# Moving the value products of the segment's tokens behind its Wo pass, with new PSUM banks for K and for the extra transposes

## Chip, cores, metric

One core of one Trainium2 chip. The metric is device time in microseconds (us), median of the runs. All runs quoted here, apart from the single look at a synthetic kernel, were in the fast state: a granted TensorE clock of 0.99 to 1.00, and times of one kernel on one chip that agree within 0.8%. The profiler's trace of one execution of each run is what the views below show.

## The reference, cut to what matters

A pre-LN block: an attention part A with a recurrent memory, then a gated feed-forward part B. Part A goes through 64 segments of 32 tokens in order. Each segment is put behind 8 memory rows; the attention's first 8 output rows are the memory of the next segment. That is the recurrence which the kernel cannot break.

```python
for s in range(n_seg):                       # 64 segments, 32 heads of 128, model width 640
    h = concatenate([mem, x[:, 32*s:32*s+32]])        # 8 + 32 rows
    q, k, v = h @ Wq, h @ Wk, h @ Wv                  # per head
    p = softmax(where(mask, q @ k.T * scale, -1e9))
    o = (p @ v) @ Wo                                  # summed over heads
    mem = o[:, :8]                                    # into the next segment
    outs.append(o[:, 8:])
h  = x + concat(outs)                        # A works on layernorm(x)
h2 = h + reglu_ffn(layernorm(h))             # part B
```

## The kernel before, the parts that matter

Every operation is recorded in one list with the tiles and PSUM banks that it reads and writes; a solver sets the semaphores. Each engine executes its operations in the order of the list, so the order of the text is the order of the engine. Key `B(n)` is a PSUM bank; two users of one bank are always ordered, readers among themselves too.

```python
BQ = (0, 1); T0, T1 = 2, 3; P0, P1, P2, P3 = 4, 5, 6, 7          # names of the 8 banks

def project(act, akeys, j, halves, banks, chunks=range(5)):      # j: 0 Q, 1 K, 2 V
    # 5 chunks x 4 column groups: a 128x32 stationary load, then a matmul of 512 columns
    # (one load serves two matmuls where both halves are asked for)

def to_act(s, wkey, src):        # memory rows of the next segment: Wo's result -> stationary operand
    add("dve", transpose(TBf, src)); add("dve", tensor_copy(act_r[..., 0:M], TBf))

def pv_x(s, b0):                 # "x values": 64 loads + 64 matmuls on 32x32 tiles
    for kh in range(2):
        for a in range(2):
            for c in range(4):
                for g in range(4):
                    pe.matmul(bank(b0 + g)[32*c:32*c+32, 129*kh:129*kh+129], Px[...], t[...])
def norm_x(b0):                  # VectorE: reciprocal (rx), two multiplies (ox), reads banks b0..b0+3

def extra_units(s):              # 3 of 4 segments also project 32 extra tokens, in pieces ("filler")
    ...
    def fin():                   # for K or Q: transposes of the result, in the next segment
        trans8(tok[2], ("tok", 2), tok[3], ("tok", 3), P0)
        (evac_k if j == 1 else evac_q)(P0, t0, 32, 0, "act")

for s in range(64):
    ...
    if s > 0:
        project(a, ks, 1, (0,), (P2,)); to_tok(P2, 0, "act")     # K, needs the memory rows
        project(a, ks, 1, (1,), (P3,)); to_tok(P3, 1, "dve")
        if fin: fin()
        pv_x(s - 1, BQ[0]); norm_x(BQ[0])                        # x values of the segment before
        ... row_scale ...
        project(a, ks, 0, (0, 1), (P0, P1)); ...                 # Q
        project(a, ks, 2, (0,), BQ[:1]); ...                     # V, first half
        trans8(... P2); trans8(... P3)                           # K and Q transposed
        project(a, ks, 2, (1,), (T0,)); ...                      # V, second half
    scores(s); exp_mem(); exp_x()                                # 64 loads + 64 matmuls, then ScalarE
    filler(0); pv_mem(s); filler(1); trans_om(s); trans_ox(s - 1, T0)
    wo_pass(oT[par], ..., T1)                                    # 128 loads + 128 matmuls, 160 columns
    to_act(s + 1, B(T1), bank(T1)[:, 0:160])
    ...
    filler(2)                                                    # extra projection or Wo of memory rows
    if evac: evac()
    ... row_stats ...
```

The softmax here doesn't subtract the row's maximum and nothing guards it: scores larger than these inputs give would overflow.

## Time and profile before

| | before |
|---|---|
| time, median of 3 | 1268.34 us (1266.53 to 1270.35) |
| span, profiled run | 1262.6 us |
| TensorE busy | 1176.5 us, 93% |
| TensorE idle for the memory copy (act_r), segments only | 12.6 us in 47 waits |
| TensorE idle for the evacuation of the extra transposes | 13.8 us in 30 waits |

The head of the page of the kernel before, and its queue of instruction transfers:

```profile
span 1262.6 us, 64636 instructions
## 1 busy us (share of the span) xinstructions
PE 1176.5 (93%) x31431; PEld 661.4 (52%) x29111; DVE 611.0 (48%) x1497; ACT 408.4 (32%) x775; POOL 26.6 (2%) x94
...
q8 instruction: 237, 3.88, 1.3%
```

PE is TensorE's matmuls, PEld its weight loads, which overlap (1176.5 and 661.4 us busy in a span of 1262.6).

The waits of TensorE in the segments, 60 to 1046 us (columns: total, times, longest):

```profile
PE ps L345 <- DVE act_r L467: 12.6, 47, 0.7
PE ps L345 <- ACT Qr L378: 7.1, 15, 0.6
PE ps L345 <- ACT Kr L378: 6.7, 15, 0.5
...
PE ps L546 <- issue: 1.7, 4, 0.6
```

L345 is the projections. The first line is K waiting for the memory rows, the next two are Q waiting for bank 4 while ScalarE reads the extra transposes from it. TensorE's timeline shows both in one segment (columns: start, duration, instruction, in brackets the idle time before it and what ended it):

```profile
301.69 0.73 PE L546 MATMUL ps<-Wo,oT 128*32 128x160 bf16 x32
302.24 0.39 PE L345 MATMUL ps<-W,act_e 128*32 128x512 bf16 x4
302.46 0.39 PE L331 MATMUL ps<-W,act_e 128*32 128x512 bf16 x4
303.09 2.34 PE L345 MATMUL ps<-W,act_r 128*32 128x512 bf16 x40 [0.24 <-DVE act_r L467]
305.36 0.62 PE L364 MATMUL ps<-ident,tok 128*128 128x128 bf16 x8
305.91 0.28 PE L583 MATMUL ps<-Vr,Px 32*32 32x129 bf16 x16
...
307.10 0.40 PE L345 MATMUL ps<-W,act_r 128*32 128x512 bf16 x4 [0.45 <-ACT Qr L378]
```

Order: end of the Wo pass (L546), filler (act_e), wait, K, extra transposes (L364), x values (L583), wait, Q.

### The profile page before, as it was taken

What the parts mean: (1) busy time and instruction counts of PE and PEld (TensorE: products, weight loads), DVE (VectorE), ACT (ScalarE), POOL (GpSimd) and SP (SyncE); (2) the same over time, 40 slices, a digit from 0 to 9 for tenths busy, and PEclk for the clock granted to TensorE, in tenths of its full rate; (3) what the DMA queues carried; (4) which work ended last, traced back from release to release, by engine and by line L of the source; (5) the groups of instructions that cost most, each with busy time, mean ns of one, the idle gap of its engine ahead of it and who ended that gap; (6) DMA issues with size and microseconds to landing.
All of it is one profiled execution on the core that took longest, in us unless ns stands there. A gap on an engine that the chain in (4) does not pass through costs nothing.

```text
span 1262.6 us, 64636 instructions
## 1 busy us (share of the span) xinstructions
PE 1176.5 (93%) x31431; PEld 661.4 (52%) x29111; DVE 611.0 (48%) x1497; ACT 408.4 (32%) x775; POOL 26.6 (2%) x94
## 2 busy tenths in 40 slices
PE   0889999999999999999999999999999997999998
PEld 0255555555556555555555555555555554455454
DVE  2244545454545454555555555454545442543522
ACT  0323333333333333333333333333333321321311
POOL 1000000000000000000000000000000000000000
PEclk9999999999999999999999999999999998999999
DMA  9801000010110101010111010100000025110100
GB/s 364 310 21 24 21 23 21 23 23 22 23 24 21 25 19 25 21 44 19 43 22 44 21 44 20 24 20 23 20 21 20 19 99 183 37 63 22 43 21 21
DMA packets 47819, 60.03 MB, mean 48 GB/s; under 512 B 20224, under 2 KB 36288, under 8 KB 47552
## 3 DMA queue, kind: packets, MB, share of 16 engines
q1 hardware_dynamic: 43520, 45.41, 12.6%
q10 hardware_dynamic: 4032, 10.49, 2.2%
q8 instruction: 237, 3.88, 1.3%
q14 instruction: 30, 0.25, 0.1%
HBM read 36.79 MB, written 6.55 MB: 34 GB/s over the span
## 4 chain that ended last, share of the span: by engine, by line
PE 86%; DMA 4%; DVE 4%; ACT 3%; issue 1%; SPq 1%; POOL 0%; DVEq 0%; ACTq 0%; POOLq 0%
PE ps L345 32%; PE ps L546 12%; PE ps L331 9%; PE ps L884 9%; PE ps L364 6%; PE ps L912 5%; PE ps L488 3%; PE ps L372 2%; PE ps L558 2%; PE ps L521 2%; DVE TBf L466 2%; DMA W<-in_A_Wk_dram 2%; PE ps L583 2%; ACT Kr L378 1%; ACT Qr L378 1%
## 5 line engine op out<-in xcount | busy, mean ns | idle before, releaser
L345 PE MATMUL ps<-W,act_r 128*32 128x512 bf16 x6460 | 447.2, 381 | 39.0 <-DVE act_r L467 12.6
L345 PEld LDWEIGHTS ps<-W,act_r 128*32 128x32 bf16 x6460 | 162.9, 96 | 286.0 <-issue 84.4
L380 DVE CAST tok<-ps 128x512 bf16<-128x512 f32 x161 | 110.9, 689 | 154.8 <-PE ps L345 78.3
L378 ACT ACTIVATE tok<-ps 128x512 bf16<-128x512 f32 x161 | 95.9, 596 | 229.7 <-PE ps L331 187.8
L546 PE MATMUL ps<-Wo,oT 128*32 128x160 bf16 x8448 | 163.8, 236 | 3.1 <-issue 2.6
L546 PEld LDWEIGHTS ps<-Wo,oT 128*32 128x32 bf16 x8448 | 148.6, 98 | 12.7 <-issue 4.5
L331 PE MATMUL ps<-W,act_r 128*32 128x512 bf16 x1420 | 138.8, 381 | 0.0
L364 PEld LDWEIGHTS ps<-ident,tok 128*128 128x128 bf16 x1288 | 72.2, 98 | 48.5 <-issue 24.2
L364 PE MATMUL ps<-ident,tok 128*128 128x128 bf16 x1288 | 89.1, 220 | 4.7 <-DVE tok L380 4.7
L604 ACT ACTIVATE oT<-ps 128x768 bf16<-128x768 bf16 x64 | 51.9, 811 | 124.4 <-PE ps L372 124.4
L345 PE MATMUL ps<-W,act_e 128*32 128x512 bf16 x900 | 89.6, 381 | 0.1
L331 PE MATMUL ps<-W,act_e 128*32 128x512 bf16 x900 | 89.2, 379 | 0.0
L378 ACT ACTIVATE Qr<-ps 128x512 bf16<-128x512 bf16 (+3 forms) x110 | 69.1, 658 | 57.4 <-DVE Qr L380 45.4
L596 DVE TENSOR_TENSOR ox<-ps,rx 128x512 bf16<-128x512 f32 x128 | 82.4, 685 | 2.2
L899 DVE TENSOR_TENSOR hT<-g,ps 128x512 bf16<-128x512 bf16 (+1 forms) x56 | 37.8, 686 | 74.7 <-PE ps L884 53.1
L466 DVE STREAM_TRANSPOSE TBf<-ps 128x160 f32<-128x160 f32 x64 | 22.4, 350 | 100.7 <-PE ps L546 100.6
L884 PE MATMUL ps<-xn2T,Wu 128*128 128x512 bf16 x260 | 66.7, 388 | 4.2 <-DMA Wu<-in_B_W_up_dram 4.2
L884 PE MATMUL ps<-xn2T,Wg 128*128 128x512 bf16 x260 | 66.6, 388 | 3.1 <-ACT g L897 3.1
L912 PE MATMUL ps<-Wd,hT 128*128 128x320 bf16 x448 | 68.1, 300 | 0.0
L378 ACT ACTIVATE wtok<-ps 128x160 bf16<-128x160 f32 x64 | 19.5, 304 | 138.7 <-DVE TBf L466 122.4
L897 ACT ACTIVATE g<-ps 128x512 bf16<-128x512 f32 (+1 forms) x56 | 32.3, 594 | 97.1 <-PE ps L884 97.1
L380 DVE CAST Vp<-ps 128x512 bf16<-128x512 f32 x64 | 44.3, 692 | 27.8 <-PE ps L345 26.4
(88 smaller groups left out, 1169.5 us busy)
## 6 DMA issues: line engine op xcount, KB each, us to landing
Vr<-Vp SPq DMA_DIRECT2D x124, 48.8 KB
xt<-in_A_x_dram SPq DMA_DIRECT2D x30, 160.0 KB
Vr<-Vp SPq DMA_DIRECT2D x128, 32.5 KB
attn_d<-wtok SPq DMA_DIRECT2D x256, 7.5 KB
W<-in_A_Wk_dram ACTq DMA_DIRECT2D x1, 2560.0 KB
W<-in_A_Wq_dram ACTq DMA_DIRECT2D x1, 2560.0 KB
W<-in_A_Wv_dram ACTq DMA_DIRECT2D x1, 2560.0 KB
Wo<-in_A_Wo_dram ACTq DMA_DIRECT2D x1, 2560.0 KB
```

Source lines behind the costliest of these rows:

```text
L331: return pe.add_instruction(mybir.InstMatmult(name=nc.get_next_instruction_name(), engine=mybir.EngineType.PE, ins=[pe.lower_ap(rhs), pe.l ...
L345: ins = pe.matmul(*a, start=(c == 0), stop=(c == DC - 1), skip_group_check=True)
L364: ins = pe.matmul(bank_bf(b)[:, k * 128:(k + 1) * 128], t[:, (k % 4) * 128:(k % 4 + 1) * 128], ident[:, :], is_transpose=True)
L378: add("act", lambda a: a.activation(dst, src, ACTF.Copy), r=r, w=w)
L380: add("dve", lambda v: v.tensor_copy(dst, src), r=r, w=w)
L466: add("dve", lambda v: v.transpose(TBf[:].rearrange("p c t -> p (c t)"), src), r=[wkey], w=[("TBf",)])
L488: i = pe.matmul(o, lh, Qr[:, h, q, :], start=True, stop=True, skip_group_check=True)
L546: i = pe.matmul(bank(bk)[32 * gg:32 * gg + 32, 0:160], src[:, hb, :], w[:, gg], start=(hb == 0), stop=(hb == 31), skip_group_check=True)
L596: add("dve", lambda v, kh=kh: v.tensor_tensor(ox[:, :, kh, :], src[:, :, kh, 0:128], ap(rx, kh, [[2, 4], [0, 128]]), ALU.mult), r=[B(b0 + ...
L604: add("act", lambda a: a.activation(oT[par][:, :, M:32].rearrange("p (k g) q -> p g k q", g=4), src[:, :, :, 0:RID], ACTF.Copy), r=[B(bk)] ...
L884: ins = pe.matmul(bank(bk), w[:, c, lo:lo + 128], xn2T[par][:, c, :], start=(c == 0), stop=(c == DC - 1))
L912: i = pe.matmul(bank(bk)[:, 0:320], hT[par][p0:128, j, u * 128:(u + 1) * 128], Wd[p0:128, j, hf * 320:(hf + 1) * 320], start=(j == 0), sto ...
```

## The change

Intent: fill the wait for the memory rows with the x values, which need nothing from them, and take the extra transposes off a bank that Q needs. Everything else follows from freeing banks. The whole diff:

```diff
--- before.py
+++ after.py
@@ -742,8 +742,8 @@
                     to_tok(BQ[i], 2 + i, e)
 
         def fin():
-            trans8(tok[2], ("tok", 2), tok[3], ("tok", 3), P0)
-            (evac_k if j == 1 else evac_q)(P0, t0, 32, 0, "act")
+            trans8(tok[2], ("tok", 2), tok[3], ("tok", 3), BQ[1])
+            (evac_k if j == 1 else evac_q)(BQ[1], t0, 32, 0, "act")
         return part, evac, (fin if j < 2 else None)
 
     EARLY = (31, 35, 39, 43)
@@ -780,22 +780,24 @@
         if s > 0:
             a, ks = pass_act(s)
             t0, nr = rider_tokens(s)
-            project(a, ks, 1, (0,), (P2,))
-            to_tok(P2, 0, "act")
-            project(a, ks, 1, (1,), (P3,))
-            to_tok(P3, 1, "dve")
+            project(a, ks, 1, (0,), (T0,))
+            to_tok(T0, 0, "act")
+            project(a, ks, 1, (1,), (T1,))
+            to_tok(T1, 1, "dve")
             if fin:
                 fin()
-            pv_x(s - 1, BQ[0])
-            norm_x(BQ[0])
+            if s % 4 == 2 and ln:
+                row_stats(xt, ("xt",), n_rows(nb))
+            if e2b is not None:
+                row_stats(xt, ("xt",), 128)
+            if not last:
+                project(a, ks, 0, (0, 1), (P0, P1))
+                to_tok(P0, 2, "act")
+                to_tok(P1, 3, "dve")
             if s % 4 == 2 and ln:
                 row_scale(xt, ("xt",), n_rows(nb), xt, ("xt",))
             if e2b is not None:
                 row_scale(xt, ("xt",), 128, at, ("at",))
-            if not last:
-                project(a, ks, 0, (0, 1), (P0, P1))
-                to_tok(P0, 2, "act")
-                to_tok(P1, 3, "dve")
             project(a, ks, 2, (0,), BQ[:1])
             to_v(BQ[0], Vp[par], 0, ("Vp", par), "act")
             trans8(tok[0], ("tok", 0), tok[1], ("tok", 1), P2)
@@ -854,17 +856,16 @@
         filler(2)
         if woe:
             copy_oTe(s - 1, T0)
+        pv_x(s, P0)
         if evac:
             evac()
+        norm_x(P0)
         if woe:
             woe_sum(BQ[0])
             woe_store(s // 4 - 1)
-        if s % 4 == 1 and ln:
-            row_stats(xt, ("xt",), n_rows(nb))
         if s % 4 == 3 and e2 is not None:
             add_attn(xt[:, :], xt, at, [("xt",), ("at",)], [("xt",)])
             dma(h_d[128 * e2:128 * e2 + 128, :], xt[:, :], r=[("xt",)], w=[("h_d", e2)])
-            row_stats(xt, ("xt",), 128)
 
 
     BG, BU, BD, BT = (0, 1), (2, 3), (4, 5), (6, 7)
```

## The prediction

> **What bounds the kernel.** TensorE: 1176.5 of 1262.6 us busy (first part of the page), 86% of the chain of waits. VectorE is 48% busy, ScalarE 32%. In the 64 recurrent segments (14.85 to 16.1 us, scores to scores in the timeline) TensorE idles at two places (its waits, 60 to 1046 us): key projection <- VectorE's memory transpose/copy (act_r), 12.6 us in 47 waits; query projection <- ScalarE's evacuation of the extra K/Q transposes, 7.1 + 6.7 us in 30; once <- VectorE's ox, 1.6 us.

> These understate the cost. [...] I measure from the last matmul start of one phase to the first start of the next: filler->K takes 0.62 us (0.43 after a Wo pass of the memory rows), x values->Q 0.67 where the extra transposes stand before it, against 0.15 where nothing is waited for. [...] here projection->x values costs 0.31, against 0.22 between four-matmul groups.

> **What the change does.** No arithmetic is added or removed. The 64 x-value matmuls (0.51 us, first to last start) move from behind K to in front of it, into the wait for act_r. The extra transposes go to bank 1, so Q on banks 4, 5 no longer waits for their 1.02 us evacuation. x values of 63 segments now use banks 4 to 7, so Q waits for the normalisation instead (0.21 + 1.29 us on VectorE), which has K's 2.2 us to hide in. K uses banks 2, 3. Layer-norm statistics (2 x 0.48 + 0.21 us) move behind it.

> **Cost by kind of segment** (filler to Q, excluding K itself and the extra transposes):
> - With extra transposes (30): before 0.62 + 0.15 + 0.51 + 0.67 = 1.95; after 0.31 + 0.51 + 0.155 + 0.15 = 1.125. Gain 0.82, 24.8 us in all.
> - After a segment with the Wo pass of memory rows (about 14): before 0.43 + 0.31 + 0.155, after 0.23 + 0.155 + 0.22. Gain 0.29, 4 us.
> - After a segment with extra V (15): nearly nothing. There VectorE's half of the V evacuation waits for ScalarE's (0.71 us idle before Vr in the timeline) and stands in front of the normalisation, which ends about 3.5 us after the filler's last start, where Q could start at 3.15. Q picks up a new wait of about 0.4 us, which eats the 0.40 gain.
> - First segments and the single long ox wait: about 3.5 us.

> Sum: 32 us, all on the critical path since TensorE sets the pace. 1268.3 - 32 = 1236 us. Range 1229 to 1246. Chances: faster by over 2% (under 1243) 0.84, within 2% 0.15, slower 0.01.

> **What would show it.** Waits of K on act_r and of Q on ScalarE's Kr/Qr evacuation both almost gone; a new wait of Q on ox, some 15 times, about 0.2 to 0.4 us; segments ending in s mod 4 = 3 and 0 falling from 16.05 and 15.92 to about 15.2 and 15.1, mod 2 from 15.1 to 14.8, mod 1 staying at 14.85. Feed-forward unchanged.

> **What would make it wrong.** VectorE running later than I lay out, so that Q waits for ox everywhere (30 more waits of 0.3 us cost 9 us); x values waiting at their new place; a lower granted clock (0.993 now); "issue" gaps turning up where waits were.

Two passages are cut from it, where the cuts are marked: the reason given for measuring from start to start, and a mechanism given for the step of 0.31 us. Neither was shown by a run of this case. The sum is 24.8 + 4 + 3.5 = 32.3, put down as 32, and the 0.31 and 0.22 us are measured in the trace before.

## The result and the profile after

The changed kernel took 1280.74 us (1277.19 to 1285.59, 4 runs) against 1267.65 us (4 runs): ratio 1.0101, 95% interval 1.0075 to 1.0128. It is slower by 1%, clear of the noise but inside the 2% either way that the prediction called "within 2%" and gave 0.15; 2.5% faster was forecast. A ratio here is that of the fast runs of the same rounds, as recorded, so it is not quite the ratio of the medians.

The head of the page after:

```profile
span 1279.7 us, 64704 instructions
## 1 busy us (share of the span) xinstructions
PE 1176.9 (92%) x31413; PEld 664.0 (52%) x29111; DVE 608.8 (48%) x1497; ACT 407.7 (32%) x775; POOL 26.6 (2%) x94
...
q8 instruction: 237, 3.88, 1.3%
```

Busy time is the same; the 17 us are idle time. TensorE's waits after, same window:

```profile
PE ps L583 <- issue: 31.2, 31, 1.7
PE ps L345 <- issue: 5.3, 10, 1.6
PE ps L546 <- issue: 4.4, 10, 0.9
PE ps L558 <- issue: 2.2, 2, 1.3
```

Both waits that the change was made against are gone, as forecast: no act_r, no Kr, no Qr in this window. In their place TensorE idles in front of the x values (L583) and elsewhere for "issue", the profile's word for waiting on nothing that it shows. The timeline after, for a segment of the same kind, shows where:

```profile
286.01 2.40 PE L546 MATMUL ps<-Wo,oT 128*32 128x160 bf16 x128
288.24 0.39 PE L345 MATMUL ps<-W,act_e 128*32 128x512 bf16 x4
288.45 0.39 PE L331 MATMUL ps<-W,act_e 128*32 128x512 bf16 x4
288.77 0.28 PE L583 MATMUL ps<-Vr,Px 32*32 32x129 bf16 x16
288.84 0.26 PE L583 MATMUL ps<-Vp,Px 8*32 8x129 bf16 x14
290.25 0.23 PE L583 MATMUL ps<-Vp,Px 8*32 8x129 bf16 x2 [1.15 <-issue]
290.25 0.28 PE L583 MATMUL ps<-Vr,Px 32*32 32x129 bf16 x16
290.32 0.41 PE L583 MATMUL ps<-Vp,Px 8*32 8x129 bf16 x16
290.66 2.34 PE L345 MATMUL ps<-W,act_r 128*32 128x512 bf16 x40
292.93 0.62 PE L364 MATMUL ps<-ident,tok 128*128 128x128 bf16 x8
293.48 0.40 PE L345 MATMUL ps<-W,act_r 128*32 128x512 bf16 x4
```

The gap falls in the middle of one recorded operation, after 30 of its 64 matmuls, where the program has no semaphore at all. Counting TensorE's instructions (loads, matmuls and the semaphore instructions between them) from the start of the trace and looking at the transfers of the instruction queue gives, for four of the gaps after:

```
gap ends   instruction number   modulo 256   last 16 KB instruction packet began   256 instructions before
258.66     11969                193          2.68 us earlier, took 1.46            3.50 us earlier
290.25     13762                194          2.30 us earlier, took 0.96            3.66 us earlier
322.01     15553                193          2.42 us earlier, took 0.92            3.64 us earlier
354.28     17346                194          2.32 us earlier, took 0.99            3.15 us earlier
```

Of the 67 issue gaps over 0.1 us in the whole trace, 58 stand at 193 or 194 modulo 256; the other nine lie in the feed-forward, where some matmul records are missing, so that the count is no longer exact. (Why 193 and not 0 is not shown; the count begins with the first recorded instruction, and all 22 issue gaps of the synthetic kernel below stand at 193 too.) All 58 end 1.2 to 1.6 us after the last 16 KB packet of the queue has ended. The queue moves 16 KB packets, 237 for TensorE's 60,848 instructions, that is one packet for 257. By these counts TensorE stands at the end of a block of 256 instructions and waits for the next.

How can the demand exceed the supply? Over a whole segment before (880 to 956 instructions in 14.85 to 16.1 us in most) 256 instructions take 4.1 us or more. But the Wo pass is 256 instructions in 2.2 us and the x values are 128 in 0.5 us (2.17 and 0.51 us from first to last matmul start, medians before). The change put them next to each other, with 32 or fewer instructions of filler between.

To weigh it, I took for every block end between 60 and 1046 us the step from one matmul start to the next, less the median of the same kind of step elsewhere, where it was larger than normal steps are. This sum is called the block-end loss below. It is 7.9 us before and 62.0 us after. The span grew by 17.1 us, so everything else became 62.0 - 7.9 - 17.1 = 37 us shorter; 32 us were forecast. This is a balance of one trace of each, and the fixed window leaves out the last segment of the slower kernel. Taken from the first scores to the last, the 63 steps grew by 15.0 us (984.7 to 999.7) and the loss from 8.1 to 64.1, which leaves 41 us. So 37 to 41 us is what the two counts give.

### The profile page after: what moved, and what is told of

It is laid out like the page before. It is cut to its first block, busy times and chain, and to the rows that moved or that the text cites. A ratio compares the mean times of both kernels' runs of the same rounds, so it can differ in the third digit from the quotient of the medians.

```text
span 1279.7 us, 64704 instructions
## 1 busy us (share of the span) xinstructions
PE 1176.9 (92%) x31413; PEld 664.0 (52%) x29111; DVE 608.8 (48%) x1497; ACT 407.7 (32%) x775; POOL 26.6 (2%) x94
## 4 chain that ended last, share of the span: by engine, by line
PE 89%; DMA 4%; issue 4%; DVE 1%; SPq 1%; ACT 0%; POOL 0%; DVEq 0%; ACTq 0%; POOLq 0%
PE ps L345 32%; PE ps L546 12%; PE ps L331 10%; PE ps L885 8%; PE ps L364 6%; PE ps L913 5%; PE ps L583 3%; PE ps L558 3%; PE ps L488 2%; PE ps L372 2%; PE ps L521 2%; DMA W<-in_A_Wk_dram 2%; SPq L304 1%; PE ps L533 1%; DMA Wd<-in_B_W_down_dram 1%
## 5 line engine op out<-in xcount | busy, mean ns | idle before, releaser
L345 PE MATMUL ps<-W,act_r 128*32 128x512 bf16 x6460 | 450.7, 383 | 14.5 <-DMA W<-in_A_Wk_dram 8.5
L345 PEld LDWEIGHTS ps<-W,act_r 128*32 128x32 bf16 x6460 | 166.8, 97 | 246.7 <-issue 103.3
L378 ACT ACTIVATE tok<-ps 128x512 bf16<-128x512 f32 x161 | 95.7, 595 | 234.8 <-PE ps L345 127.6
L546 PEld LDWEIGHTS ps<-Wo,oT 128*32 128x32 bf16 x8448 | 147.4, 97 | 17.1 <-issue 8.9
L331 PE MATMUL ps<-W,act_r 128*32 128x512 bf16 x1420 | 142.9, 385 | 0.0
L378 ACT ACTIVATE Qr<-ps 128x512 bf16<-128x512 bf16 (+3 forms) x110 | 69.2, 658 | 62.7 <-DVE Qr L380 45.5
L885 PE MATMUL ps<-xn2T,Wg 128*128 128x512 bf16 x250 | 62.5, 379 | 3.9 <-ACT g L898 2.5
L378 ACT ACTIVATE wtok<-ps 128x160 bf16<-128x160 f32 x64 | 19.5, 304 | 142.2 <-DVE TBf L466 125.2
L583 PE MATMUL ps<-Vp,Px 8*32 8x129 bf16 x2048 | 42.7, 222 | 20.3 <-issue 20.3
```

The source lines that it names most:

```text
L331: return pe.add_instruction(mybir.InstMatmult(name=nc.get_next_instruction_name(), engine=mybir.EngineType.PE, ins=[pe.lower_ap(rhs), pe.l ...
L345: ins = pe.matmul(*a, start=(c == 0), stop=(c == DC - 1), skip_group_check=True)
L378: add("act", lambda a: a.activation(dst, src, ACTF.Copy), r=r, w=w)
L546: i = pe.matmul(bank(bk)[32 * gg:32 * gg + 32, 0:160], src[:, hb, :], w[:, gg], start=(hb == 0), stop=(hb == 31), skip_group_check=True)
L583: i = pe.matmul(bank(b0 + g)[32 * c:32 * c + 32, 129 * kh:129 * kh + 129], Px[32 * g:32 * g + n, 256 * a + 32 * k:256 * a + 32 * k + 32], ...
L885: ins = pe.matmul(bank(bk), w[:, c, lo:lo + 128], xn2T[par][:, c, :], start=(c == 0), stop=(c == DC - 1))
```

## Experiments

| run | what | time us | before, same chip | ratio | block-end loss us |
|---|---|---|---|---|---|
| e2_after_shift128 | after, stream shifted by half a block | 1270.31 | 1264.24 | 1.0047 | 53.7 |
| e3_before_shift128 | before, shifted likewise | 1268.04 | 1267.91 | 1.0009 | 11.1 |
| e4_after_half_loads | after, 64 loads fewer in each Wo pass | 1234.18 | 1264.24 | 0.9755 | 17.3 |
| e5_before_half_loads | before, likewise | 1255.73 | 1264.24 | 0.9928 | 0 |
| e6_move_only | after, extra transposes back on bank 4 | 1307.01 | 1267.91 | 1.0311 | 51.4 |
| e1_fin_bank6 | before, extra transposes on bank 6 | 1255.15 | 1264.24 | 0.9924 | 9.7 |
| e8_bank6_stats | e1 with the statistics moved | 1256.25 | 1265.62 | 0.9915 | 15.9 |
| e9_split_memory | e8 with the memory copy in two pieces | 1251.25 | 1265.62 | 0.9882 | 17.7 |
| e10_k_joint | after, 20 loads fewer in each K | 1274.99 | 1267.26 | 1.0052 | 54.6 |
| e11_after_again | after, unedited | 1282.32 | 1267.26 | 1.0112 | 62.9 |

### The supply by itself

A kernel in which TensorE runs alone on zeros (result wrong on purpose; one run of 285.0 us, its state unknown, mean granted clock 0.927): stretches of 1024 loads and 1024 matmuls of 160, 224, 288 and 352 columns between slow stretches, then a burst in the form of the x values, then 160 columns again beside small DMAs.

```diff
+for N in (160, 224, 288, 352):        # each after 192 slow matmuls of 512 columns
+    for r in range(256):
+        for g in range(4):
+            pe.matmul(bank(b)[32*g:32*g+32, 0:N], oT[0][:, r % 32, :], wsrc[:, 0:N], ...)
+for r in range(32): ...               # 512 matmuls on 32x32 tiles, 129 columns
```

> TensorE alone (output zeros on purpose): stretches of load + matmul pairs whose matmuls stream 160, 224, 288 and 352 columns in four column groups, which unhindered need 2.2, 3.0, 3.9 and 4.7 us per 256 instructions, between slow stretches of 512 columns; then a burst like the x values (1.0 us per 256), then 160 columns again while small DMAs run. Supply theory: the 160-column stretch runs at a block time of 3.0 to 3.6 us in place of 2.2, 224 at the same, 288 and 352 at their own pace without gaps, the burst at 3.0 to 3.6 us per 256 after a first part that runs free, and 160 with DMA traffic somewhat slower, 3.3 to 4.0. Rival (no such limit; the gaps of the changed kernel are its own): 2.2 us for 160 columns, 1.0 for the burst.

The unhindered times in it are estimates: the Wo pass before, 160 columns, took 2.17 us for 256 instructions, which scaled by columns gives 2.2, 3.0, 3.9 and 4.8; the 1.0 of the burst is twice the 0.51 us of the x values.

The stretches in the view by groups (L321: 160 columns, L335: 224, L349: 288, L363: 352, L378: burst, L397: 160 with DMA traffic; columns: busy, mean ns, idle before):

```profile
L363 PE MATMUL ps<-Wo,oT 128*32 128x352 bf16 x1024 | 38.4, 313 | 0.0
L349 PE MATMUL ps<-Wo,oT 128*32 128x288 bf16 x1024 | 31.6, 286 | 0.0
L335 PE MATMUL ps<-Wo,oT 128*32 128x224 bf16 x1024 | 25.9, 259 | 2.9 <-issue 2.9
L321 PE MATMUL ps<-Wo,oT 128*32 128x160 bf16 x1024 | 19.2, 233 | 7.7 <-issue 7.7
L397 PE MATMUL ps<-Wo,oT 128*32 128x160 bf16 x1024 | 19.2, 233 | 8.5 <-issue 8.5
...
L378 PE MATMUL ps<-Vp,Px 32*32 32x129 bf16 x512 | 5.4, 250 | 7.3 <-issue 7.3
```

And the burst in the timeline:

```profile
184.45 1.52 PE L378 MATMUL ps<-Vp,Px 32*32 32x129 bf16 x159
188.24 1.26 PE L378 MATMUL ps<-Vp,Px 32*32 32x129 bf16 x128 [2.27 <-issue]
192.25 1.46 PE L378 MATMUL ps<-Vp,Px 32*32 32x129 bf16 x128 [2.74 <-issue]
195.97 1.16 PE L378 MATMUL ps<-Vp,Px 32*32 32x129 bf16 x97 [2.27 <-issue]
```

The first 159 matmuls and their loads run free; then exactly 128 matmuls, 256 instructions, come every 3.7 to 4.0 us, though they are busy for 1.3 to 1.5. The free part is 319 instructions in the trace, the 63 left of the current block and one more block. Stretches whose own pace is slower than that (288 columns: 3.9 us per 256, 352: 4.8) have no gap; 224 columns (about 3.1 on its own, worked out from the two slower stretches) is held at 3.6 on average, 160 columns (about 2.2, as in the Wo pass before) at 3.4, free first part included. These averages agree with the expectation, but the blocks that follow the free part do not quite: by the gaps in the trace they came every 3.45 to 3.73 us at 160 columns and every 3.45 to 4.00 us at 224, and those of the burst every 3.7 to 4.0 us, where 3.0 to 3.6 had been expected. (The granted clock was 0.76 in the window of the burst and 1.00 in the 160-column stretch; whether that lengthened the block times of the burst was not shown.) DMA traffic added 0.1 us per block on average, so contention is not the cause: the gaps are there with no other DMA running (from 184 to 197.2 us, the burst, the DMA view shows 4 packets, all of the instruction queue).

### Alignment

The same padding in front of both kernels, in time when TensorE idles anyway:

```diff
+def pad(pe):
+    for _ in range(64):
+        i = pe.matmul(bank(P3)[:, 0:32], ident[:, :], ident[:, 0:32], start=True, stop=True, ...)
+    return i
+add("pe", pad, r=[("ident",)], w=[B(P3)])
```

> The changed kernel with 128 more TensorE instructions (64 small matmuls on an unused bank) in the idle time before the weights arrive, so that every later TensorE instruction stands half a block of 256 further on in the instruction stream. Theory (instruction supply: blocks of 256 TensorE instructions arrive no faster than about one in 3.3 us, and the stretch Wo pass + filler + x values asks for more): the total stays at 1281 us within 8 us, and the issue gaps move from instruction count 193 modulo 256 to about 65 modulo 256. Rival (unlucky alignment of the blocks with the segments, which both repeat every 3584 instructions): the time falls to 1235 to 1255 us. Rival (the gaps are hidden waits for a semaphore or a DMA at the new place of the x values): the gaps stay at the same instructions of the segment and the time stays.

> The kernel before with the same 128 instructions in front. Supply theory: 1268 us within 6 us, its few issue gaps at about 65 modulo 256. Rival (the kernel before is fast by a lucky alignment): 1280 us or more.

> The changed kernel, unedited, on the same chip as the run beside it: ratio to before 1.010 as first measured (1.007 to 1.013), some 50 to 60 us of stalls at block ends. If the ratio falls to 1.005 here, the 7 us that the shift by 128 instructions seemed to win were the chip's.

The gaps of the shifted kernel stand at other instructions of the segments and, counted with the padding, still at 193 and 194 modulo 256 (the expectation's 65 holds only without counting it). The changed kernel lost 62.9 us at block ends unshifted (e11) and 53.7 us shifted; ratios 1.0112 (1.0074 to 1.0150) and 1.0047 (1.0018 to 1.0076), on two chips. My bound of 8 us around 1281 was missed: the shift is worth some 7 to 9 us in the changed kernel, though the two intervals just touch, and why is open. Alignment is not the cause of the loss: the shift did not bring the 1235 to 1255 us of that rival, most of the loss stays, and the kernel before does not care (1.0009).

The trace after settles this rival without any run. In it four segments are 3634 instructions in most cases (3643 in others), and not the 3584 of the expectation, which would be exactly 14 blocks. So the block ends move on by about 50 instructions every four segments, and one run meets many alignments in turn: the gaps in the x values stand anywhere between the matmul numbered 1 and the one numbered 62, counted from 0 to 63. (That the gaps in the list above are 1791 to 1793 instructions apart says only that each stands at a block end.) This also speaks against a hidden wait at one instruction of the x values.

### Fewer instructions in the burst

Every second group of loads is left out of the Wo pass (the arithmetic is wrong). Same matmuls, 64 of 256 instructions fewer.

```diff
     for gg in range(4):
+        if hb % 2:
+            i = again(pe, bank(bk)[...], src[:, hb - 1, :], w[:, gg], False, hb == 31, gg)   # no load
+            continue
         i = pe.matmul(bank(bk)[32 * gg:32 * gg + 32, 0:160], src[:, hb, :], w[:, gg], ...)
```

> The changed kernel with every second group of weight loads left out of the Wo pass (64 of its 256 instructions; result wrong on purpose; matmuls and their sizes as before). Supply theory: replaying the trace with those instructions taken out and a block per 3.2 to 3.4 us leaves 18 to 27 us of stalls in place of 46 to 59, so about 1252 us (1243 to 1262). Rival (hidden wait at the x values, or slower x values on banks 4 to 7): the gaps stay, 1275 us or more.

> Control: the same loads left out of the kernel before (result wrong on purpose). Supply theory: only the few stalls that the kernel before has go, 5 to 10 us: 1258 to 1264 us. If the loads themselves cost TensorE time, it falls by as much as the changed kernel does, 28 us, to about 1240.

TensorE's waits of the changed kernel without those loads, in the segments (L587 is the x values there):

```profile
PE ps L587 <- issue: 6.7, 13, 0.9
...
PE ps L345 <- issue: 1.0, 3, 0.4
PE ps L550 <- issue: 0.5, 1, 0.5
```

The changed kernel fell from 1.0101 of before, as first measured, to 0.9755, 1234 us; its span is 45.4 us shorter and its block-end loss 44.7 us smaller. The control lost 8.5 us, about what its block ends had cost (7.9). So by these two numbers the loads themselves cost TensorE almost nothing here; what they cost is their place in the stream. The time fell below the expected 1243 to 1262 us, so the range was missed: 17.3 us of block-end loss were left, just under what my replay gave (18 to 27 us), but it had started the changed kernel at 46 to 59 us, too low. This is also the strongest check of the forecast: with the supply relieved, the change is worth 1255.73 - 1234.18 = 21.6 us over the kernel before with the same loads left out, with 17.3 us still lost at block ends, and 32 us were forecast. That 1234 us is close to the 1236 us forecast for the change itself is chance: this kernel has fewer loads. Slower x values on banks 4 to 7 and a hidden wait are ruled out by it: neither would go away with loads of another operation.

### Fewer instructions elsewhere

```diff
-            project(a, ks, 1, (0,), (T0,))
-            to_tok(T0, 0, "act")
-            project(a, ks, 1, (1,), (T1,))
+            project(a, ks, 1, (0, 1), (T0, T1))
+            to_tok(T0, 0, "act")
             to_tok(T1, 1, "dve")
```

> The changed kernel with both halves of K projected together, so that 20 weight loads of each segment (1260 of 60848 instructions) go, as in the half-load run, but in the slow K stretch and not in the Wo pass; the result stays right. Theory (what counts is the local demand in the burst): nothing won, replay of the trace gives 1 us less; within 6 us of the unchanged changed kernel beside it. Rival (the total number of instructions counts, 45 us for 4224 loads in the half-load run): 13 us less than the run beside it.

1274.99 us beside 1282.32 us: 7.3 us less, between the two expectations (within 6 us, or 13 us). Block-end loss 54.6 instead of 62.9. It does not settle the matter: the intervals of the two ratios overlap (1.0008 to 1.0096 beside 1.0074 to 1.0150), and the loss is about that of the shifted kernel (53.7), which has all its loads. Whether the 7 us are a rate effect or of the same unexplained kind as those of the shift, no run shows. Per load removed it won about half of what the loads of the Wo pass won.

### One part of the change at a time

The move alone: after, with the extra transposes back on P0 (bank 4).

```diff
-            trans8(tok[2], ("tok", 2), tok[3], ("tok", 3), BQ[1])
-            (evac_k if j == 1 else evac_q)(BQ[1], t0, 32, 0, "act")
+            trans8(tok[2], ("tok", 2), tok[3], ("tok", 3), P0)
+            (evac_k if j == 1 else evac_q)(P0, t0, 32, 0, "act")
```

> The changed kernel with the extra transposes back on bank 4 (x values moved, K on banks 2 and 3 as changed). Q waits for their evacuation again, 30 times about 0.5 us; this wait stands behind the stalls of the x values, which stay: 1281 + 15 = 1296 us (1288 to 1300). If the waits give the supply time to catch up, it stays near 1281.

```profile
PE ps L583 <- issue: 23.4, 28, 1.6
PE ps L345 <- ACT Kr L378: 16.7, 15, 1.1
PE ps L345 <- ACT Qr L378: 16.7, 15, 1.1
PE ps L345 <- issue: 8.5, 13, 1.7
```

1307 us: worse than expected. I had carried over the 0.5 us wait from before; but there the x values stood between transposes and Q and hid half of the evacuation. With them gone it is 1.1 us, 33.4 us in all. The two parts of the change belong together. The block-end loss fell by 11 us to 51.4 (over all segments by about 8, as this kernel runs further past the window), which would fit that waits give the supply some time.

The bank alone: before, with the extra transposes on bank 6, free by then because ScalarE has read the first half of K.

```diff
-            trans8(tok[2], ("tok", 2), tok[3], ("tok", 3), P0)
-            (evac_k if j == 1 else evac_q)(P0, t0, 32, 0, "act")
+            trans8(tok[2], ("tok", 2), tok[3], ("tok", 3), P2)
+            (evac_k if j == 1 else evac_q)(P2, t0, 32, 0, "act")
```

> The kernel before with one part of the change in another form: the extra K/Q transposes go to bank 6 (free once ScalarE has read the first half of K) in place of bank 4, so Q no longer waits for their evacuation; order of TensorE's instructions untouched. Theory: 30 waits of 0.52 us go (0.67 to 0.15 us from x values to Q), 15.6 us, and because x values stay apart from the Wo pass at most 4 us of new supply stalls come: 1252 us (1250 to 1258), the fastest kernel so far. Rival (any denser TensorE stream pays the gain back in supply stalls): 1262 us or more.

```profile
PE ps L345 <- DVE act_r L467: 12.7, 47, 0.7
PE ps L364 <- ACT tok L378: 3.8, 4, 1.0
```

1255.15 us, 9 us faster than before, inside the expected 1250 to 1258. Q's waits are gone; four new waits of 1.0 us came where the layer-norm statistics hold ScalarE and with it the first half of K. Block ends cost 9.7 us, 2 more than before. So this denser TensorE stream was hardly punished (2 us); the one with the burst was (54 us).

### Two steps further

Statistics behind the x values' normalisation, as in the change (against the bank-6 kernel; the two calls at the end of the segment go):

```diff
             norm_x(BQ[0])
+            if s % 4 == 2 and ln:
+                row_stats(xt, ("xt",), n_rows(nb))
+            if e2b is not None:
+                row_stats(xt, ("xt",), 128)
-            ... row_scale ...
             project(a, ks, 0, (0, 1), (P0, P1)); to_tok(...); to_tok(...)
+            ... row_scale ...
```

> The bank-6 kernel (extra transposes on bank 6, order of TensorE untouched) with the layer-norm statistics behind the x values' normalisation, and their scaling behind Q's evacuations, as the change has them. In the bank-6 kernel four segments of 16.7 to 17.4 us (against 15.4) lose 1.0 us each because ScalarE reads K late, held by the statistics, and the transposes to bank 6 wait for it. Theory: those four fall to about 15.5, 5 to 6 us in all: ratio to before about 0.988, 1249 us (1246 to 1253). Rival: the statistics now delay Q's evacuation or the scores and nothing is won: ratio 0.992 or more.

Missed: 1256.25 us, ratio 0.9915 against 0.9924, no difference. The four waits of 1.0 us (3.8 us in all) are gone from the profile, but block ends cost 15.9 us instead of 9.7: by these traces the instruction supply took back what the waits gave. Then the memory copy in two pieces, so that K's first chunks start early:

```diff
-        add("dve", transpose(TBf, src)); add("dve", tensor_copy(act_r[..., 0:M], TBf))
+        for lo, hi in ((0, 2), (2, 5)):
+            add("dve", transpose(TBf[:, lo:hi], src[:, 32*lo:32*hi])); add("dve", tensor_copy(act_r[lo:hi], ...))
-            project(a, ks, 1, (0,), (P2,))
+            project(a, ks_first_piece, 1, (0,), (P2,), range(0, 2))
+            project(a, ks, 1, (0,), (P2,), range(2, 5))
```

> The kernel of the run beside it, with the memory's transpose and copy on VectorE in two pieces (chunks 0 to 1, then 2 to 4), so that K can start on the first piece. Theory: K starts 0.15 to 0.2 us earlier in 47 segments, 7 to 9 us, and the stream is still slack enough for the instruction supply: ratio to before about 0.982, 1242 us (1238 to 1248). Rival (supply takes back what any earlier start wins): no faster than the run beside it, more issue gaps.

```profile
PE ps L345 <- DVE act_r L469: 1.7, 3, 0.6
```

1251.25 us, ratio 0.9882 (0.9853 to 0.9911): outside the expected 1238 to 1248. The waits for act_r fell from 12.6 us in 47 to 1.7 us in 3, K starts 0.62 -> 0.51 us after the filler's last start, 0.11 us less and not the 0.15 to 0.2 expected, 5 us in all; 5.0 us is what the median fell, but the interval of the ratio overlaps that of the run beside it (0.9893 to 0.9937). It has the lowest median of the correct kernels, 1.2% under before, and its block ends already cost 17.7 us. More of this kind is likely to meet the same limit.

## Why the prediction was wrong, point by point

- "What bounds the kernel: TensorE" held, and both idle places were the right ones. The change removed both completely.
- "With extra transposes (30): ... Gain 0.82" and the other terms by kind of segment: right in sum, a little low. Without the block-end loss the segments gained 37 to 41 us by the balance above; 32 were forecast. Kind by kind, the scores-to-scores times after, each less its own block-end loss (medians), are 15.20, 15.09 and 14.71 us for the segments ending in s mod 4 = 3, 0 and 2, where "about 15.2 and 15.1" and 14.8 were forecast; s mod 4 = 1 came to 14.4 where 14.85 was forecast to stay. So the terms held, and none of them was the step that failed.
- "Q picks up a new wait of about 0.4 us" (after a segment with extra V): right in kind, smaller. In the run with fewer loads the step from K to Q in those segments is 0.51 us in 8 of them, against 0.22 without a wait, so 0.3 us; in the changed kernel as such it shows in 3, most likely because the supply stalls come first and give VectorE time.
- "Sum: 32 us, all on the critical path since TensorE sets the pace": this is the step that failed. It took for granted that TensorE, once nothing makes it wait, runs through the new order at the step times measured in the old one. The step times of the x values and of the Wo pass had been measured with a slow K projection between them. Side by side they ask for 256 instructions in about 2 us; at the 58 gaps after, the last 256 had taken 3.6 us in the median. The block-end loss rose by 54 us, more than the change saved.
- "x values ... into the wait for act_r": the wait was not only lost time. It stood just behind the densest stretch of the stream, the Wo pass, and with the wait left in place (bank alone, e1) block ends cost 9.7 us, not 62. That the wait, with K behind it, gave the instruction supply time to catch up is my reading; no run shows it by itself.
- "'issue' gaps turning up where waits were" was named as a way to be wrong, but given no size. The number was to be had from the trace of before: nine such gaps, all at 193 or 194 modulo 256, one of them 1.27 us long.
- "projection->x values costs 0.31": the step is there after as before, 45 of 45 times after the filler. This term was right.

## What to carry to other kernels

In these kernels TensorE's own instruction stream had a rate: once the free part was used up, 256 instructions took about 3.5 to 4 us in the synthetic kernel (3.7 to 4.0 in the burst), and 3.6 us in the median at the 58 gaps after. Before packing short TensorE instructions together, count them over the densest window of 256, loads included: where the window takes less than that, a gain from removed waits may come back as "issue" gaps that lie multiples of 256 instructions apart, as here (block-end loss 7.9 us before, 62.0 after). Dropping 64 loads from each dense Wo pass won 45 us, and removing Q's waits alone (e1) won 9 us with 2 us more lost at block ends; so try changes of these two kinds first, and look at where the instruction-queue packets fall before believing that a wait is free time.
